# Loading alpha, q and k four tokens a run for the first nine units, and turning them by half-width products instead of transposes

## The chip, the cores and the metric

The kernel runs on one core of a Trainium2 chip. The metric is the device time of one execution in microseconds (us). Before the change the median of three executions is 540.11 us (539.74 to 540.44). The traces are of single executions taken by the hardware profiler; their clock starts at the span's start.

## The reference

Two stages. A gated linear attention over batch 4, heads 8, 768 tokens, head size 48, and then a feed-forward network on the 3072 rows of 384 channels that it makes.

```python
for t in range(S):
    state = alpha[:, :, t, :, None] * state + np.einsum('bhd,bhe->bhde', k[:, :, t], v[:, :, t])
    y[:, :, t] = np.einsum('bhd,bhde->bhe', q[:, :, t], state)
x = y.transpose(0, 2, 1, 3).reshape(B * S, H * D)
h = x @ w_in            # 384 -> 2048
g = np.maximum(0.01 * h, h)
out = g @ w_out         # 2048 -> 384
```

All is float32. alpha lies between 0.8 and 1.

## The kernel before, in words

**Units.** The tokens are cut into chunks of 128, and a unit is one chunk of one batch with its 8 heads: 24 units, numbered so that units 0 to 3 are the first chunk of the four batches, 4 to 7 the second, and so on. Three units make a block of 384 rows for the feed-forward network; there are 8 blocks. The first nine units (`AHEAD` = 9) run alone at the start, from 0 to about 60 us, since the network has nothing to do before block 0 is there; the later 15 units are strewn between the matrix products of the network.

**One unit.** alpha, q and k come from HBM, and must stand with the channel on the partition and the token along the free dimension, so that a running product over tokens is a scan along a row. In the first nine units the loads put a token on each partition and the 8 heads side by side (`by_token`, pitch 64 per head, 48 of them data and 16 ones); TensorE turns them: `transposed` issues four transposes of 128 columns, each of two heads, into one bank of PSUM (L272). In later units the load puts runs of four tokens on a partition and VectorE turns the data (L284), which the change does not touch. Then:

- `scans`: VectorE (DVE) makes the running product of alpha per head pair (`pc`, L309, four scans), reciprocals of every 16th (L311), and a scan backwards for the scaled inverses (`rc`, L315); GpSimd (POOL) copies two small columns (L319, L314).
- `scaled_q`, `scaled_k`: DVE multiplies the turned q by `pc` (L334) and the turned k by `rc` (L342).
- `scores`: eight products of 48 rows on TensorE (PE, L351), two at a time in the two halves of the array's rows, into an `a` and a `b` bank; ScalarE (ACT) copies them out (L361), POOL zeroes what lies above the diagonal (L362).
- `k_tokens`: four transposes of the scaled k (L374) and an ACT copy (L376).
- `outputs`: products of the state with q (only from unit 4 on), of the masked scores with v (L390; each has 64 or 48 stationary columns and they run in pairs, one in each half of the array's columns) and of k with v for the next state (L411). ACT rounds the result into the network's input (L419), DVE the remainder (L420).
- `next_state`: `us` (L430, L432) and the POOL product L367.

A float32 product is two passes and shows as two records in the trace; a transpose is one record.

**What sets the order.** The program writes units overlapped (`attention`): turning alpha of unit u+1 comes ahead of the scores of u, turning its q and k between the scores and the outputs of u. Within that, a list scheduler of the framework orders each engine's queue at build time by its own estimate of durations, so a change of instructions moves others too. Each engine executes its queue strictly in that order. Banks of PSUM come from two rotating sets of three (`a`, `b`). SyncE (SP) issues all loads; eight of them can be under way, since each takes one of eight semaphores in turn.

**Around the change.** Loads of alpha, q, k are double buffered: the load for u+2 waits until u has been turned. v has three buffers. The conversion of the network's weights from float32 words (ACT L238, L246; DVE L240, L243, L250, L252, L254, L257) starts inside the last of the nine units for f = 0 and 1. `keep_warm` issues products on zeros into an unused bank, so that PE isn't idle in the first 10 us: two per second transpose of alpha and q of unit 0, and for k of unit 0 two products of 512 and two of 256 columns (`keep_warm_wide`, L167). From about 76 us on, PE runs the network's products (L487, L512) nearly without a gap to the end.

## Time and profile before

| | |
|---|---|
| median of three executions | 540.11 us |
| profiled execution | 538.77 us, span 537.1 us, so 1.67 us outside the span |
| PE busy | 518.8 us, 97% of the span |
| DVE / ACT / POOL busy | 375.0 / 234.0 / 49.1 us |
| first nine units | 0 to about 60 us |
| time at which unit 1, 5, 6, 7, 8 begin their scan L309 | 9.86, 32.05, 39.15, 45.84, 52.78 us |
| loads of alpha, q, k of the first nine units | 192 KB each, runs of 192 bytes |

Busy time on PE counts a product from its start to its modelled end, and pipelined products overlap, so a step of the stream is read from the distance of starts and not from a duration. PE is the engine that matters after 76 us; before that, five engines wait for each other in a cycle per unit, and the distance between the same instruction of two successive units is the length of a cycle.

### The profile page before, as it was taken

What the parts mean: (1) busy time and instruction counts of PE and PEld (TensorE: products, weight loads), DVE (VectorE), ACT (ScalarE), POOL (GpSimd) and SP (SyncE); (2) the same over time, 40 slices, a digit from 0 to 9 for tenths busy, and PEclk for the clock granted to TensorE, in tenths of its full rate; (3) what the DMA queues carried; (4) which work ended last, traced back from release to release, by engine and by line L of the source; (5) the groups of instructions that cost most, each with busy time, mean ns of one, the idle gap of its engine ahead of it and who ended that gap; (6) DMA issues with size and microseconds to landing.
All of it is one profiled execution on the core that took longest, in us unless ns stands there. A gap on an engine that the chain in (4) does not pass through costs nothing.

```text
span 537.1 us, 10383 instructions
## 1 busy us (share of the span) xinstructions
PE 518.8 (97%) x3934; PEld 492.6 (92%) x3934; DVE 375.0 (70%) x703; ACT 234.0 (44%) x514; POOL 49.1 (9%) x116
## 2 busy tenths in 40 slices
PE   8879899999999999999999999999999999999995
PEld 7668789999999899999999999999999999999995
DVE  6778999999988897875675685775777534332331
ACT  2665755555533453435334443344343354233331
POOL 3333510000000011010000001000000000000000
PEclk9999899999999999999999999999999999999998
DMA  9999854454823643533323422523201010001001
GB/s 149 163 179 183 198 140 119 117 131 136 183 53 87 190 117 78 107 81 98 70 67 70 108 69 64 98 50 92 71 0 38 11 35 1 22 1 45 1 1 49
DMA packets 92985, 46.67 MB, mean 87 GB/s; under 512 B 57856, under 2 KB 90112, under 8 KB 92928
## 3 DMA queue, kind: packets, MB, share of 16 engines
q1 hardware_dynamic: 92928, 45.93, 39.0%
q8 instruction: 33, 0.54, 0.4%
q14 instruction: 24, 0.20, 0.1%
HBM read 38.83 MB, written 4.72 MB: 81 GB/s over the span
## 4 chain that ended last, share of the span: by engine, by line
PE 86%; DVE 4%; DMA 3%; issue 2%; ACT 1%; SPq 1%; POOL 1%; ACTq 0%; DVEq 0%; POOLq 0%
PE ph L487 36%; PE b L512 32%; PE a L390 5%; PE a L351 4%; PE a L512 4%; DMA small<-in_alpha_dram 2%; DMA raw<-in_moe_w_in_dram 1%; PE a L374 1%; PE b L272 1%; PE a L411 1%; PE b L390 1%; DVE pc L309 1%; PE b L411 1%; POOL sm L362 1%; DVE rc L315 0%
## 5 line engine op out<-in xcount | busy, mean ns | idle before, releaser
L487 PE MATMUL ph<-large,w 128*128 128x384 f32 x1152 | 227.4, 340 | 2.8 <-DVE t L493 2.8
L487 PEld LDWEIGHTS ph<-large,w 128*128 128x128 f32 x1152 | 201.9, 189 | 5.5 <-DVE t L493 3.9
L512 PE MATMUL b<-w,gh 128*128 128x384 f32 x672 | 170.0, 340 | 0.0
L493 DVE TENSOR_TENSOR t<-ph,t 128x384 f32<-128x384 f32 x128 | 70.5, 551 | 88.7 <-ACT t L490 88.4
L512 PEld LDWEIGHTS b<-w,gh 128*128 128x128 f32 x672 | 119.7, 188 | 2.2 <-issue 0.5
L490 ACT ACTIVATE t<-ph 128x384 f32<-128x384 f32 x128 | 62.6, 489 | 130.1 <-PE ph L487 122.8
L495 ACT CAST gh<-t 128x384 fp32r<-128x384 f32 x128 | 65.7, 514 | 112.8 <-DVE t L493 102.6
L512 PE MATMUL b<-w,gl 128*128 128x384 f32 x336 | 107.4, 336 | 0.0
L499 DVE TENSOR_TENSOR gl<-t,gh 128x384 fp32r<-128x384 f32 x128 | 70.8, 553 | 34.4 <-ACT gh L495 33.2
L512 PEld LDWEIGHTS b<-w,gl 128*128 128x128 f32 x336 | 62.5, 188 | 0.1
L362 POOL TENSOR_SCALAR_AFFINE_SELECT sm<-sm 128x512 f32<-128x512 f32 x33 | 22.8, 705 | 113.3 <-ACT sm L361 113.3
L351 PE MATMUL a<-qs,ks 48*128 48x128 f32 x312 | 30.9, 287 | 0.1
L351 PEld LDWEIGHTS a<-qs,ks 48*128 48x128 f32 x312 | 25.9, 189 | 5.4 <-issue 4.4
L284 DVE STREAM_TRANSPOSE ks<-small 128x512 f32<-128x512 f32 x15 | 16.6, 1121 | 12.3 <-PE a L374 12.3
L390 PE MATMUL a<-sm,small 128*48 128x128 f32 (+1 forms) x312 | 23.2, 282 | 0.1
L319 POOL COPY pe<-pc 128x4 f32<-128x4 f32 x24 | 4.8, 202 | 188.6 <-DVE pc L309 188.6
L309 DVE TENSOR_TENSOR_SCAN pc<-e,small 128x128 f32<-128x128 f32 x60 | 20.1, 398 | 0.5 <-ACT pc L327 0.5
L367 POOL TENSOR_TENSOR small<-us,pe 112x192 f32<-112x192 f32 x20 | 11.9, 594 | 90.2 <-DVE us L432 87.5
L390 PEld LDWEIGHTS a<-sm,small 128*48 128x48 f32 (+1 forms) x312 | 17.1, 132 | 3.2 <-issue 3.0
L361 ACT COPY sm<-a 128x512 f32<-128x512 f32 x24 | 14.0, 585 | 13.8 <-PE b L351 11.1
L512 PE MATMUL a<-w,gh 128*128 128x384 f32 x96 | 20.0, 336 | 0.0
L315 DVE TENSOR_TENSOR_SCAN rc<-e,small 128x511 f32<-128x511 f32 x15 | 19.0, 1270 | 0.2
(86 smaller groups left out, 525.4 us busy)
## 6 DMA issues: line engine op xcount, KB each, us to landing
raw<-in_moe_w_out_dram SPq DMA_DIRECT2D x16, 384.0 KB, 3.9
small<-in_v_dram SPq DMA_DIRECT2D x24, 192.0 KB, 4.0
raw<-in_moe_w_in_dram SPq DMA_DIRECT2D x32, 144.0 KB, 3.9
out_dram<-t SPq DMA_DIRECT2D x24, 192.0 KB, 1.9
small<-in_alpha_dram SPq DMA_DIRECT2D x32, 96.0 KB, 2.3
small<-in_q_dram SPq DMA_DIRECT2D x30, 96.0 KB, 2.2
small<-in_k_dram SPq DMA_DIRECT2D x30, 96.0 KB, 2.2
small<-in_alpha_dram SPq DMA_DIRECT2D x30, 80.0 KB, 2.3
```

Of the source, the lines that this page charges most:

```text
L284: nc.vector.transpose(t.rearrange("r p (j t) -> r p t j", t=T4), src.rearrange("r p (t d) -> r p t d", t=T4)[:, :, :, 0:32],)
L309: nc.vector.tensor_tensor_scan(pc[:, p, :], aT[:, p, :], ones.broadcast_to([P, C]), 1.0, ALU.mult, ALU.mult)
L315: nc.vector.tensor_tensor_scan(flat[2][:, NP * C - 2::-1], flat[0][:, NP * C - 1:0:-1], flat[1][:, NP * C - 2::-1], last, ALU.mult, ALU.add)
L351: nc.tensor.matmul(ss[s][:, p, :], ks[lo:lo + D, p, :], qs[lo:lo + D, p, :], start=True, stop=True)
L362: nc.gpsimd.affine_select(out=sm[s], in_=sm[s], compare_op=ALU.is_ge, fill=0.0, base=0, pattern=[[0, NP], [1, C]], channel_multiplier=-1)
L390: nc.tensor.matmul(y[s][HB * c:HB * c + lhsT.shape[-1], p % 2, :], lhsT, rhs, skip_group_check=True, **kw)
L487: nc.tensor.matmul(ph, w_in_of(f, wn, g), xt[:, g, :], start=n == 0, stop=n == 3 * NG - 1)
L490: put(ordered, "ACT", lambda: nc.scalar.mul(t, ph, 0.01))
L493: put(ordered, "DVE", lambda: nc.vector.tensor_tensor(t, ph, t, ALU.max))
L495: put(ordered, "ACT", lambda: nc.scalar.copy(gh, t))
L499: made["gl", i, f] = put(ordered, "DVE", lambda: nc.vector.tensor_tensor(gl, t, gh.bitcast(F32), ALU.subtract))
L512: nc.tensor.matmul(po[j], gt[:, js], w_out_of(f, wn), start=f == 0 and n == 0, stop=f == NF - 1 and n == 2)
```

## The change

For the first nine units each load of alpha, q or k becomes two loads (heads 0, 2, 4, 6 and heads 1, 3, 5, 7). A partition now holds four successive tokens of one head, 768 bytes in one run; partition 32p + j holds tokens 4j to 4j+3 of head pair p. The two halves of a tile lie `PITCH` = 208 elements apart, of which 16 at the end are ones (`tails`).

To turn such a tile, the kernel issues for each of the four tokens n of a run, and each half s, a product of 64 stationary columns (`src[:, at:at + HB]`: the 48 channels of that token and the 16 next elements) with the identity. The result goes into the PSUM partitions 64s to 64s+63 and into every fourth column, n, n+4, n+8 and so on, so that after the eight products column t of pair p is token t as before. It is a plain product, not a transpose, so each is two passes.

The zeros tile with its memset, and the wide products on it, are dropped; with k of unit 0 go four ordinary `keep_warm` products. The memset of the gaps on DVE covers 32 elements per row in place of 128, that of the rest on POOL 416 in place of 320.

```diff
         if u < AHEAD:
-            n = H if u or i else H // 2
-            for h in range(0, H, n):
+            for s in (0, 1):
                 nc.sync.dma_start(
-                    by_token(t)[:, h:h + n, 0:D], src[b, h:h + n, ts, :].rearrange("h t d -> t h d")
+                    t[:, s * PITCH:s * PITCH + RUN],
+                    src[b, s::2, ts, :].rearrange("p (j t) d -> p j (t d)", t=T4),
                 )
             return
...
-    zeros = cst.tile([P, 4 * C], F32R, name="zeros")
-    nc.gpsimd.memset(zeros.bitcast(F32), 0.0)
...
+    def tails(t):
+        return t[:, 0:2 * PITCH].rearrange("r (s n) -> r s n", s=2)[:, :, RUN:]
...
-            nc.vector.memset(by_token(t)[:, :, D:], 1.0)
+            nc.vector.memset(tails(t), 1.0)
...
-            nc.gpsimd.memset(t[:, H * HB:], 1.0)
+            nc.gpsimd.memset(t[:, 2 * PITCH:], 1.0)
...
         if u < AHEAD:
-            ps = banks4()
-            for p in range(NP):
-                last = nc.tensor.transpose(
-                    ps[:, p, :], by_token(src)[:, 2 * p:2 * p + 2, :].rearrange("t h d -> t (h d)"), ident
-                )
-                if u == 0 and p % 2:
+            ps = bank()
+            for n in range(T4):
+                for s in (0, 1):
+                    at = s * PITCH + n * D
+                    last = nc.tensor.matmul(
+                        ps[HB * s:HB * (s + 1), n::T4], src[:, at:at + HB], ident, start=True, stop=True, skip_group_check=True
+                    )
+                if u == 0 and n % 2:
                     with tc.issue_after(last.ins):
-                        if i == 2:
-                            keep_warm_wide(4 * C if p == 1 else 2 * C)
-                        else:
-                            keep_warm(2)
-            return ps
+                        keep_warm(2)
+            return ps.rearrange("r (p t) -> r p t", p=NP)
```

Since the scheduler orders the queues anew, more moves than the diff tells. Three places are shown. In a row, `L272 MATMUL a_113<-small_73 128x128 x2` is two instructions of line 272 that read the tile small_73 (all small tiles and the loads are parts of it) and write bank a_113; rows count program instructions, so a float32 product is one row here and two records in the trace. After the change line 272 is line 270, 162 is 160, 351 is 346, 374 is 369, 390 is 385, 411 is 406.

PE at the very start, up to the scores of unit 0. Before:

```order
L162 MATMUL ph_79<-small_73 128x128 x6
L272 MATMUL a_113<-small_73 128x128 x2
L162 MATMUL ph_79<-small_73 128x128 x2
L272 MATMUL a_113<-small_73 128x128 x2
L162 MATMUL ph_79<-small_73 128x128 x2
L272 MATMUL b_135<-small_73 128x128 x4
L272 MATMUL a_147<-small_73 128x128 x4
L272 MATMUL b_160<-small_73 128x128 x4
L162 MATMUL ph_79<-small_73 128x128 x4
L167 MATMUL ph_79<-zeros_77 128x512 x2
L167 MATMUL ph_79<-zeros_77 128x256 x2
L351 MATMUL a_178<-qs_145,ks_157 128x128
```

And of the change:

```order
L160 MATMUL ph_77<-small_73 128x128 x6
L270 MATMUL a_116<-small_73 64x128
L270 MATMUL b_143<-small_73 64x128
L270 MATMUL a_116<-small_73 64x128 x3
L160 MATMUL ph_77<-small_73 128x128 x2
L270 MATMUL a_116<-small_73 64x128 x4
L160 MATMUL ph_77<-small_73 128x128 x2
L270 MATMUL b_143<-small_73 64x128 x7
L270 MATMUL a_160<-small_73 64x128 x8
L270 MATMUL b_178<-small_73 64x128 x6
L160 MATMUL ph_77<-small_73 128x128 x8
L270 MATMUL b_178<-small_73 64x128 x2
```

The four banks that are turned here are alpha, q and k of unit 0 and alpha of unit 1. The first product of q stands between those of alpha, and the last two products of unit 1's alpha now stand behind eight `keep_warm` products.

PE in the cycle of unit 1, from the transposes of its scaled k on. Before:

```order
L374 MATMUL a_279<-small_73,ks_217 128x112 x4
L272 MATMUL b_288<-small_73 128x128 x4
L272 MATMUL a_296<-small_73 128x128 x4
L390 MATMUL b_304<-sm_272,small_73 64x128
L390 MATMUL b_304<-sm_272,small_73 48x128
L390 MATMUL b_304<-sm_272,small_73 64x128
L390 MATMUL b_304<-sm_272,small_73 48x128
L272 MATMUL b_331<-small_73 128x128 x4
L411 MATMUL b_304<-small_73,ktok_284 64x48
L411 MATMUL b_304<-small_73,ktok_284 48x48
```

And of the change:

```order
L369 MATMUL a_317<-small_73,ks_250 128x112 x4
L270 MATMUL a_339<-small_73 64x128 x2
L270 MATMUL b_326<-small_73 64x128 x8
L270 MATMUL a_339<-small_73 64x128 x6
L385 MATMUL b_352<-sm_310,small_73 64x128
L385 MATMUL b_352<-sm_310,small_73 48x128
L385 MATMUL b_352<-sm_310,small_73 64x128
L385 MATMUL b_352<-sm_310,small_73 48x128
L270 MATMUL b_379<-small_73 64x128
L406 MATMUL b_352<-small_73,ktok_322 64x48
L406 MATMUL b_352<-small_73,ktok_322 48x48
L385 MATMUL a_353<-sm_311,small_73 64x128
```

q and k of unit 2 (banks b_288, a_296, now b_326, a_339) take sixteen products in place of eight transposes. Of alpha of unit 3 (b_331, now b_379) one product stays where the four transposes were; the other seven now come behind the last L406, right ahead of the scores of unit 2.

DVE from the scaled k of unit 7 to that of unit 8, where the conversion of the weights f = 0 is mixed in. Before:

```order
L240 TENSOR_SCALAR bits<-raw 128x768
L243 SCALAR_TENSOR_TENSOR bits<-raw,bits 128x768
L309 SCALAR_TENSOR_TENSOR pc<-b,small 128x128 x4
L250 TENSOR_SCALAR pw<-bits 128x768
L310 MEMSET b 128x32
L311 RECIPROCAL small<-pc 128x32
L252 TENSOR_TENSOR bits<-bits,w_770 128x768
L254 SCALAR_TENSOR_TENSOR pw<-raw,pw 128x768
L315 SCALAR_TENSOR_TENSOR rc<-b,small 128x511
```

And of the change (L236 to L253 are L240 to L257 of before, L304 is L309, L415 is L420, L427 is L432):

```order
L236 TENSOR_SCALAR bits<-raw 128x768
L239 SCALAR_TENSOR_TENSOR bits<-raw,bits 128x768
L246 TENSOR_SCALAR pw<-bits 128x768
L415 TENSOR_TENSOR large<-a,large 112x2x128
L250 SCALAR_TENSOR_TENSOR pw<-raw,pw 128x768
L248 TENSOR_TENSOR bits<-bits,w_890 128x768
L304 SCALAR_TENSOR_TENSOR pc<-b,small 128x128 x4
L415 TENSOR_TENSOR large<-b,large 112x2x128
L427 TENSOR_TENSOR us<-small,b 112x192
L253 TENSOR_TENSOR w_890<-pw,bits 128x768
L305 MEMSET b 128x32
L306 RECIPROCAL small<-pc 128x32
```

The conversion now comes nearly whole ahead of unit 8's scan. In units 0 to 6 the two L420 of a unit, which before stood around the reciprocal L311 or behind the scan L315 of the next unit, now stand behind its L342. Behind unit 8 the queues of ACT, POOL and DVE are the same as before but for single neighbours.

More of the change, by code (lines that the diff above doesn't have):

```diff
@@ L162, in keep_warm @@
             nc.tensor.matmul(idle[:, 0:C], seed[:, 0, :], seed[:, 1, :], start=True, stop=True)
-    def keep_warm_wide(n):
-        for _ in range(2):
-            nc.tensor.matmul(idle[:, 0:n], zeros[:, 0:P], zeros[:, 0:n], start=True, stop=True)
     keep_warm(6)
+    def tails(t):
+        return t[:, 0:2 * PITCH].rearrange("r (s n) -> r s n", s=2)[:, :, RUN:]
     for i in (0, 1, 2):
         for t in loads_sb[i]:
-            nc.vector.memset(by_token(t)[:, :, D:], 1.0)
+            nc.vector.memset(tails(t), 1.0)
     for n in range(max(NL)):
```

## The prediction

> **What bounds the kernel now.** I began with the windows, cut where units 2, 3, 4, 5, 6, 7, 8 begin their scan L309 and where the network begins. The columns are the stretch, its length, the busy time of PE, PE's weight loads, DVE, ACT and POOL with their instructions, the granted clock of PE, the DMA share and GB/s.
>
> ```profile
> 15.21:20.82 5.61, 4.79 (x70) 3.92 (x69) 4.67 (x11) 3.75 (x10) 2.06 (x5) 1.00 1.30 154
> 26.43:32.05 5.62, 4.79 (x71) 3.92 (x69) 4.67 (x12) 3.80 (x11) 2.06 (x5) 1.00 0.92 187
> 32.05:39.15 7.10, 5.11 (x76) 3.98 (x75) 4.88 (x12) 3.94 (x11) 2.07 (x5) 1.00 0.99 173
> 39.15:45.84 6.69, 6.69 (x84) 5.97 (x82) 5.16 (x13) 3.94 (x11) 2.10 (x5) 0.75 1.21 180
> 45.84:52.78 6.94, 6.63 (x109) 5.61 (x108) 6.72 (x14) 3.56 (x11) 2.38 (x5) 1.00 0.90 178
> 45.84:69.91 24.07, 22.22 (x280) 18.70 (x278) 22.91 (x44) 15.79 (x39) 9.53 (x13) 0.93 0.92 202
> 76.40:537.10 460.70, 453.05 (x3192) 436.61 (x3192) 312.19 (x568) 192.98 (x416) 22.82 (x56) 1.00 0.30 73
> ```
>
> From 76.4 us PE is busy for 453.05 of 460.70 us, with work that the change leaves alone. So the change is worth what it moves the 76.4 us, no more and no less. Ahead of that no engine is full in a cycle of 5.61 us, and the DMA share is around 1 (overlapping packets count twice). The waits of 15 to 33 us say who holds the cycle:
>
> ```profile
> DVE pc L309 <- PE b L272: 3.6, 4, 1.0
> PE b L390 <- POOL sm L362: 2.5, 3, 0.8
> ```
>
> The two alternate: PE waits 0.8 us a cycle for POOL's masked scores, DVE 0.9 us for the turned alpha, which stands behind that wait in PE's queue. One cycle of PE and its ends, from the timeline (start, length, engine, line):
>
> ```profile
> 20.06 0.66 PE L272 MATMUL b<-small 128*128 128x128 f32 x4
> 20.64 0.61 PE L411 MATMUL b<-small,ktok 128*64 128x48 f32 x15
> 20.82 1.36 DVE L309 TENSOR_TENSOR_SCAN pc<-b,small 128x128 f32<-128x128 f32 x4 [0.86 <-PE b L272]
> 21.05 0.30 PE L390 MATMUL a<-sm,small 128*48 128x128 f32 x1
> 21.69 0.37 PE L351 MATMUL a<-qs,ks 48*128 48x128 f32 x1
> 22.57 0.27 PE L351 MATMUL a<-qs,ks 48*128 48x128 f32 x1
> 22.78 0.60 PE L374 MATMUL a<-small,ks 112*128 112x112 f32 x4
> 23.22 0.60 PE L272 MATMUL b<-small 128*128 128x128 f32 x4
> 23.66 0.60 PE L272 MATMUL a<-small 128*128 128x128 f32 x4
> 25.09 0.65 PE L390 MATMUL b<-sm,small 128*64 128x128 f32 x8 [0.83 <-POOL sm L362]
> ```
>
> Starts give the steps: four transposes 0.44 us (23.22 to 23.66), 0.58 with the change of shape behind them (20.06 to 20.64). The scores, eight products in pairs, two passes each, are eight steps of 0.107 with 0.21 for the first, and 1.09 to the next kind (21.69 to 22.78).
>
> **What is removed, added, moved.**
>
> *The new turn.* Eight products of two passes, in pairs on the two halves of the columns. No row shows one. The nearest is L390: the same 64 stationary columns, 128 moving ones, 128 rows, in pairs:
>
> ```profile
> 50.06 0.32 PE L390 MATMUL b<-qs,small 48*64 48x128 f32 x2
> 50.67 0.66 PE L272 MATMUL b<-small 128*128 128x128 f32 x4
> 51.26 0.65 PE L390 MATMUL b<-sm,small 128*64 128x128 f32 x8
> 51.74 0.27 PE L411 MATMUL b<-small,ktok 128*48 128x48 f32 x4
> ```
>
> Eight records take 0.48 us to the next kind (51.26 to 51.74): four steps of 0.107 and 0.05, against 0.15 behind transposes. So a bank costs 16 records, 0.86 us, for 0.44: 0.42 more on PE, 27 times. Bounds: a pair that doesn't overlap costs 1.72 a bank; cheaper than 0.86 no row allows. I take 0.86, the row being the same form but for the strided target.
>
> *A cycle of the first chunk* (units 1 to 4 in the scans; PE only): scores 1.09, L374 0.54, q and k 16 steps and a first step 1.81, switch 0.05, L390 0.48, one product of alpha alone 0.26 (two steps and a switch), first L411 0.10, L390 0.48, rest of L411 0.32, seven products of alpha 1.03 (0.21, six steps of 0.107, and 0.18 to the scores). Sum 6.16. POOL's wait is gone: its result lets L390 go 3.40 us after the scores begin (21.69 to 25.09), and PE's own queue now comes to L390 after 1.09 + 0.54 + 1.81 + 0.05 = 3.49. DVE, busy 4.67 us a cycle, is not full. So PE becomes the bound: 4 × 6.16 = 24.64 us against 22.19 from 9.86 to 32.05: **+2.45**. Bounds: 5.61, if it doesn't push (+0.25), to 6.57, if each switch costs the 0.15 to 0.20 of the transposes (+4.1).
>
> *Cycles with a state* (units 4 and 5): scores 1.09, L374 0.54, q and k 1.81, switch 0.05, state products 0.58 (0.61 at 50.06), L390 0.91, L411 0.43, alpha 1.04: 6.45. Before they took 7.10 and 6.69. The first held ACT in a wait for weights, the second ran at clock 0.75:
>
> ```profile
> ACT raw L238 <- DMA raw<-in_moe_w_in_dram: 2.6, 1, 2.6
> DMA to landing us min/median/max: 2.4/4.9/7.4
> DMA to landing us min/median/max: 1.9/2.2/3.8
> L128 SPq DMA_DIRECT2D small<-in_q_dram x9: 378/912/2311, 1.9 to 49.3; - x9
> L135 SPq DMA_DIRECT2D small<-in_q_dram x60: 311/430/1652, 136.4 to 384.6; - x60
> ```
>
> The last four rows are the loads' landing and SP's issue, of L128 (192-byte runs) and of L135 (768-byte runs, the new form). Two loads at 0.43 cost SP what one at 0.91 did, and in the cycle of 6.2 us SP's six and one v fit; but they land in 2.2 and not 4.9 us, so the weights, which stand behind v of unit 5 on SP, are there before ACT asks. With PE full I take clock 1.00. 2 × 6.45 − 13.79 = **−0.89** (bounds −1.6 at 6.1 a cycle, +1.9 if one of them runs at 0.75, 6.45 / 0.75 = 8.6).
>
> The Trainium skill, "TensorE: Matmul & The Clock Gate", Part 4, says that transposes don't count as activity for the clock gate as products do; by it the new products would make the 0.75 stretch less likely. The stretch of 15.21 to 32.05 has 36 transposes at 1.00, so the rows don't show it; by the rule −0.89 stands, without it +1.9 is open.
>
> *The start.* The rows of before:
>
> ```profile
> 4.25 0.64 PE L272 MATMUL a<-small 128*128 128x128 f32 x2
> 4.68 0.75 PE L162 MATMUL ph<-small 128*128 128x128 f32 x4
> 5.27 0.38 PE L272 MATMUL a<-small 128*128 128x128 f32 x2
> 5.69 1.36 DVE L309 TENSOR_TENSOR_SCAN pc<-a,small 128x128 f32<-128x128 f32 x4 [3.36 <-PE a L272]
> 8.17 1.06 PE L162 MATMUL ph<-small 128*128 128x128 f32 x8
> 8.98 0.94 PE L167 MATMUL ph<-zeros 128*128 128x512 f32 x4
> 9.86 1.35 DVE L309 TENSOR_TENSOR_SCAN pc<-b,small 128x128 f32<-128x128 f32 x4
> 10.00 0.37 PE L351 MATMUL a<-qs,ks 48*128 48x128 f32 x1
> ```
>
> PE begins at 4.25 either way, when the first six keep-warm products are through. Steps take 0.21 there up to about 5.3, and 0.11 behind. Alpha of unit 0 needs about ten steps (the first three products don't pair) and four of L160 (0.6 with switches): 4.25 + 1.05 + 0.55 + 0.6 + 0.2 to the reader = 6.65, against 5.69. Then, on PE: the other L160 0.6, q 0.96, k 0.86, six of alpha 0.65, eight L160 of two records 1.9, two of alpha 0.3, so the scores begin near 11.7 and the scan of unit 1 with them, against 9.86 to 10.00. Through DVE (6.65 and the 4.2 us from the first scan to the second) it would be 10.9. What hides the wide products today (PE waits for DVE's L342 until 10.00) doesn't hide the new L160, since alpha stands behind them. I take **+1.6** (bounds +0.4, if loads and pairing give half of it back, to +2.0).
>
> *Waits for loads that vanish.* The second cycle lost 1.2 us to alpha of unit 2, of this in all:
>
> ```profile
> PE b L272 <- DMA small<-in_alpha_dram: 1.7, 2, 1.2
> ```
>
> Its cycle of 5.35 is in the 22.19 already, and PE's 6.16 stands over it. So the gain is swallowed. The Trainium skill, "DMA: Bandwidth & Descriptors", Specifications, gives 512 bytes as the least size for full rate; by it alone the loads would be the gain, −1.7 us from this row. The 2.2 against 4.9 us agree on the loads, not on the path.
>
> *The conversions.* From unit 7's scan (45.84) to the end of the second L499 (69.91) DVE is busy 22.91 of 24.07 us. The same instructions now come in another order, with the conversion ahead of unit 8's scan. The most that a late start can win back is 1.16, all of DVE's idle time; I take **−0.8** (bounds −1.16 to 0). Behind it, DVE goes on full, and PE waits for it until 76.4.
>
> The memsets, on POOL and DVE ahead of 3.7 us, lie beside the first keep-warm products; uncovered they would cost 0.6 us.
>
> **Sum**: 1.6 + 2.45 − 0.89 − 0.8 = +2.36, so 2.4. The profiled execution would be 538.77 + 2.4 = 541.2; it lies 1.34 under the median of 540.11. On the median: **542.5 us**. All low bounds together give −2.1 (0.4 + 0.25 − 1.6 − 1.16), all high ones +8.0 (2.0 + 4.1 + 1.9); the latter needs three at once.
>
> **Rivals.**
>
> 1. *Faster: the room that PE has in a cycle takes the new products.* Place: the wait for POOL ahead of L390, 0.83 us, with 0.15 per switch that the equal shape of the turn and L390 saves. It decides if PE's cycle comes to 5.55, its mean today. Then 0.9 − 0 − 1.6 − 0.8 = −1.5: 538.6. For it: PE waits 0.83 today and is busy 4.79 of 5.61. Against it: 3 × 0.42 is 1.26, more than 0.83. Chance 0.15.
> 2. *No change: half of it.* The start costs 0.9 (through DVE only), the cycles 5.8 (+1.0) and 6.25 (−1.3), the conversions give 0.8: −0.2, 539.9. For it: the long DVE path of the start. Chance 0.23.
> 3. *The pairs don't overlap*, through the strided target or the shared identity: 0.86 more a bank, 3 × 0.86 × 6 cycles and 4 × 0.86 at the start, some 19 on the forecast: 561. Against it: L390 pairs. Chance 0.04.
> 4. The loads may not be what is waited for at all; that is in the forecast.
>
> **How the numbers follow.** The forecast has 0.58. A measurement of this kernel tells about 0.2% (1.08 us) from no change. Above +1.08 lie the forecast and rival 3, 0.62 less what of the forecast falls short of 1.08, say 0.03, and 0.01 of rival 2; I say 0.60 slower. Within: 0.24. Below −1.08: 0.16. The range runs from −0.8 (into rival 2 and the edge of rival 1) to +4.7 (forecast with one more high bound): 539.3 to 544.8. The forecast's own is 541.2 to 544.8.
>
> **What would show it.** The distance of unit scans L304 in the first chunk: 6.1 to 6.3 confirms, 5.6 is rival 1, over 8 rival 3. PE's wait for POOL ahead of L385 gone, a new wait of DVE's L304 for PE. A group L270 of 432 records, whose steps are 0.107 a pair. The first scan at 6.4 to 6.8 and the second at 11 to 12; at 10 the start was misjudged. No wait of ACT L234 for weights. Wrong altogether, if the network's steady run begins ahead of 76.4.

## The result, and the profile after

The changed kernel takes 568.98 us, the median of four executions (567.77 to 569.65). The kernel before takes 539.92 us on the same chip (538.89 to 540.44). The ratio is 1.054, with a 95% interval of 1.051 to 1.056. Slower was forecast, but by 2.4 us; it is 29 us, and the time lies 24 us above the upper end of the range. The profiled execution took 568.45 us (before: 538.77).

From the page of the changed kernel (span 566.7 us), the rows in 40 slices for the DMA engines: busy tenths, and what they moved in GB/s.

```profile
DMA  2344467444465165334333233143211010001001
GB/s 81 104 123 110 128 148 192 115 130 113 117 180 123 26 187 140 93 79 82 106 73 87 51 108 90 28 87 91 68 42 35 1 43 1 22 0 44 0 1 47
```

A slice is 14 us. Through the first five of them, 71 us, the DMA engines are busy to two to four tenths and they move 81 to 128 GB/s. The loads of alpha, q and k of the first eight units are all issued there; the six loads of the ninth follow from 71.72 to 76.4 us.

The windows of the changed kernel (columns as in the prediction: stretch, length, PE, its weight loads, DVE, ACT and POOL, granted clock, DMA share, GB/s), cut at the scans L304 of units 1 and 2, 3 and 4, 4 and 5, and at the network's steady run:

```profile
0.00:10.00 10.00, 7.54 (x34) 5.59 (x35) 0.74 (x8) 1.28 (x1) 3.40 (x14) 1.00 0.20 65
16.94:22.75 5.81, 5.81 (x102) 5.38 (x102) 4.86 (x11) 3.44 (x9) 1.54 (x4) 1.00 0.40 109
29.11:39.06 9.95, 7.67 (x102) 6.95 (x102) 5.06 (x12) 3.76 (x10) 2.05 (x5) 0.83 0.44 114
39.06:55.53 16.47, 10.50 (x152) 8.79 (x152) 5.03 (x13) 4.46 (x11) 2.05 (x5) 1.00 0.47 122
105.37:566.70 461.33, 453.04 (x3192) 436.63 (x3192) 312.00 (x568) 193.54 (x416) 22.82 (x56) 1.00 0.28 73
```

The first of these stretches, 0 to 10 us, in the kernel before:

```profile
0.00:10.00 10.00, 7.88 (x49) 7.15 (x49) 5.54 (x18) 1.28 (x1) 3.74 (x17) 1.00 1.01 138
```

The steady run now begins at 105.37 us, where it began at 76.40, and takes 461.33 us to the end of the span for 460.70. So the loss lies ahead of it. In the first 10 us the DMA share fell from 1.01 to 0.20 and the rate from 138 to 65 GB/s. That is with no engine of the core full: DVE is busy for 0.74 us of the ten.

The unit scans on DVE (units 0, 1, 4, 5 and 7 of the changed kernel):

```profile
10.14 1.37 DVE L304 TENSOR_TENSOR_SCAN pc<-a,small 128x128 f32<-128x128 f32 x4 [8.42 <-PE a L270]
...
16.94 1.36 DVE L304 TENSOR_TENSOR_SCAN pc<-b,small 128x128 f32<-128x128 f32 x4 [1.21 <-PE b L270]
...
39.06 1.37 DVE L304 TENSOR_TENSOR_SCAN pc<-b,small 128x128 f32<-128x128 f32 x4
...
55.53 1.36 DVE L304 TENSOR_TENSOR_SCAN pc<-b,small 128x128 f32<-128x128 f32 x4
...
70.85 1.36 DVE L304 TENSOR_TENSOR_SCAN pc<-b,small 128x128 f32<-128x128 f32 x4
```

From unit 1 to unit 2 the cycle is 5.81 us, with PE full. From unit 4 to unit 5 it is 16.47. The first products of the turn, on PE's timeline, and two of the waits up to 90 us (total, times, longest):

```profile
4.62 0.66 PE L270 MATMUL a<-small 128*64 128x128 f32 x2 [0.16 <-DMA small<-in_alpha_dram]
...
6.75 1.12 PE L270 MATMUL a<-small 128*64 128x128 f32 x6 [0.40 <-DMA small<-in_alpha_dram]
```

```profile
ACT raw L234 <- DMA raw<-in_moe_w_in_dram: 11.5, 2, 10.8
...
PE a L270 <- DMA small<-in_k_dram: 8.3, 7, 2.3
```

PE takes each new tile of the start when its load lands. ACT waits once for 10.8 us, for weights. Pieces of the chain of waits (start, length) show which transfers set the end:

```profile
2.24 4.46 DMA small<-in_alpha_dram
...
38.82 6.49 DMA small<-in_alpha_dram
...
50.10 3.49 DMA raw<-in_moe_w_in_dram
...
76.38 7.86 DMA small<-in_k_dram
```

The load that is issued at 2.24 us lands 4.46 us later, and later ones take 6.49 and 7.86 us. ACT's wait is behind them. SP issues the weights' loads L198 from 46.50 us on, behind the slow loads in its own order, and L234 gets its data at 53.69:

```profile
53.69 0.88 ACT L234 ACTIVATE raw<-raw 128x768 f32<-128x768 f32 x1 [10.76 <-DMA raw<-in_moe_w_in_dram]
```

```profile
L198 SPq DMA_DIRECT2D raw<-in_moe_w_in_dram x64: 312/564/2355, 46.5 to 162.6; - x64
```

Behind L234 on ACT stand the casts L414 of the unit in hand, so a unit's cycle stops with it. That is the 16.47 us.

### The profile page after: what moved, and what is told of

Its sections match the earlier page's. It is cut to its first block, busy times and chain, and to the rows that moved or that the text cites. A ratio compares the mean times of both kernels' runs of the same rounds, so it can differ in the third digit from the quotient of the medians.

```text
span 566.7 us, 11062 instructions
## 1 busy us (share of the span) xinstructions
PE 539.6 (95%) x4262; PEld 511.1 (90%) x4262; DVE 375.3 (66%) x703; ACT 234.5 (41%) x514; POOL 48.2 (9%) x115
## 4 chain that ended last, share of the span: by engine, by line
PE 86%; DMA 6%; DVE 3%; SPq 1%; issue 1%; ACT 1%; ACTq 0%; DVEq 0%
PE ph L482 34%; PE b L507 31%; PE a L385 6%; PE a L346 4%; PE a L507 4%; PE b L270 3%; DMA small<-in_k_dram 2%; DMA small<-in_alpha_dram 2%; PE a L270 2%; DMA raw<-in_moe_w_in_dram 1%; PE a L369 1%; PE b L385 1%; SPq L198 1%; PE a L406 1%; PE ph L160 1%
## 5 line engine op out<-in xcount | busy, mean ns | idle before, releaser
L482 PE MATMUL ph<-large,w 128*128 128x384 f32 x1152 | 226.1, 338 | 2.9 <-DVE t L488 2.9
L482 PEld LDWEIGHTS ph<-large,w 128*128 128x128 f32 x1152 | 200.7, 188 | 5.6 <-DVE t L488 3.8
L488 DVE TENSOR_TENSOR t<-ph,t 128x384 f32<-128x384 f32 x128 | 70.5, 551 | 88.0 <-ACT t L485 87.8
L270 PE MATMUL b<-small 128*64 128x128 f32 x272 | 25.5, 305 | 2.6 <-DMA small<-in_alpha_dram 2.1
L415 DVE TENSOR_TENSOR large<-a,large 112x256 fp32r<-112x256 f32 x39 | 15.2, 417 | 17.2 <-ACT large L414 17.2
L270 PE MATMUL a<-small 128*64 128x128 f32 x160 | 18.1, 317 | 8.9 <-DMA small<-in_k_dram 8.3
L279 DVE STREAM_TRANSPOSE ks<-small 128x512 f32<-128x512 f32 x15 | 16.7, 1127 | 13.3 <-PE a L369 13.3
L270 PEld LDWEIGHTS b<-small 128*64 128x64 f32 x272 | 19.8, 155 | 5.0 <-issue 2.5
L270 PEld LDWEIGHTS a<-small 128*64 128x64 f32 x160 | 13.5, 160 | 11.7 <-DMA small<-in_k_dram 6.6
L385 PE MATMUL a<-sm,small 128*64 128x128 f32 (+1 forms) x312 | 23.9, 282 | 0.0
L414 ACT CAST large<-a 112x256 fp32r<-112x256 f32 x39 | 13.6, 372 | 24.6 <-PE a L385 24.2
L362 POOL TENSOR_TENSOR small<-us,pe 112x192 f32<-112x192 f32 x20 | 13.2, 660 | 124.3 <-DVE us L427 90.2
```

What stands on the lines that cost most here:

```text
L270: last = nc.tensor.matmul(ps[HB * s:HB * (s + 1), n::T4], src[:, at:at + HB], ident, start=True, stop=True, skip_group_check=True)
L279: nc.vector.transpose(t.rearrange("r p (j t) -> r p t j", t=T4), src.rearrange("r p (t d) -> r p t d", t=T4)[:, :, :, 0:32],)
L385: nc.tensor.matmul(y[s][HB * c:HB * c + lhsT.shape[-1], p % 2, :], lhsT, rhs, skip_group_check=True, **kw)
L415: made["x", u] = nc.vector.tensor_tensor(xl, y[s][0:BR], xh.bitcast(F32), ALU.subtract)
L482: nc.tensor.matmul(ph, w_in_of(f, wn, g), xt[:, g, :], start=n == 0, stop=n == 3 * NG - 1)
L488: put(ordered, "DVE", lambda: nc.vector.tensor_tensor(t, ph, t, ALU.max))
```

## The experiments

**Theory 1** says that a load whose outermost dimension is four is carried by four of the sixteen DMA engines. The changed loads have the four heads outermost; those of the kernel before have 128 tokens there. **Theory 2** blames the number of loads, 54 in place of 28, with SP's issue and the semaphores. **Theory 3** blames the new products on PE and the order that they force. The kernels that were compared:

| kernel | loads of the first nine units | turn | median us | ratio to before, 95% |
|---|---|---|---|---|
| before | 128 tokens outermost, 192-byte runs | 4 transposes | 539.92 | |
| after | 4 heads outermost, 768-byte runs | 8 products | 568.98 | 1.051 to 1.056 |
| e1 | 32 runs outermost, 768-byte runs | 8 products | 546.41 | 1.010 to 1.016 |
| e2 | 8 heads outermost, 768-byte runs | 8 products | 546.55 | 1.010 to 1.016 |
| e3 | as before | 8 products | 545.58 | 1.007 to 1.013 |
| e4 | as after | 4 transposes | 565.81 | 1.046 to 1.052 |
| e5 | as e1 | 4 transposes | 542.62 | 1.003 to 1.007 |
| e6 | as e1, no keep-warm products between | 8 products | 545.25 | 1.007 to 1.012 |
| e7 | as before, two loads a tensor and unit | 4 transposes | 539.62 | 0.999 to 1.002 |
| e8 | 2 heads outermost, 768-byte runs | 8 products | 625.78 | one execution |
| e9 | as e1, one DVE step less ahead of the network | 8 products | 543.84 | 1.006 to 1.011 |
| e10 | as before, one DVE step more there | 4 transposes | 541.01 | 1.003 to 1.006 |

### e1: the same loads, with the runs outermost

```diff
-                    src[b, s::2, ts, :].rearrange("p (j t) d -> p j (t d)", t=T4),
+                    src[b, s::2, ts, :].rearrange("p (a t) d -> a p (t d)", a=JA, t=T4),
...
-                        ps[HB * s:HB * (s + 1), n::T4], src[:, at:at + HB], ident, ...
+                        ps[HB * s:HB * (s + 1), n::T4], src[:, at:at + HB], turn, ...
```

`JA` is 32. `turn` is an identity with its columns in the order of the rows; two instructions on POOL at the start make it.

> Only the loads of the first nine units differ from the changed kernel: the same 768-byte runs, the same number of loads, but the 32 runs of four tokens are the outermost dimension of the source and the four heads the inner one. A partition then holds another run, and a permuted identity in the new products puts the columns back; order and number of instructions on every engine but POOL (two more at the start) are the same. Theory 1 (a load whose outermost dimension is four is carried by four of the sixteen DMA engines: the changed kernel shows a share of 0.20 and 65 GB/s in its first 10 us) expects a share of 0.5 or more and 120 GB/s or more there, the first scan L304 near 6.7 us, the network's steady run near 78 us and 540 to 545 us. Theory 2 (twice as many loads: their issue on SP and the semaphores they share) expects no change, 566 to 571, since the loads are as many. Theory 3 (the new products on PE and the order that they force) expects 566 to 571 too.

Measured: 546.41 us (544.1 to 550.08), 22.6 less than the changed kernel. Its windows, and the group of its loads of alpha with the landing times of all of them:

```profile
0.00:10.00 10.00, 8.47 (x72) 7.49 (x74) 3.00 (x16) 1.28 (x1) 5.05 (x18) 1.00 0.45 118
19.01:24.85 5.84, 5.84 (x102) 5.41 (x102) 4.84 (x12) 3.76 (x10) 2.05 (x5) 1.00 0.60 144
```

```profile
L127 SPq DMA_DIRECT2D small<-in_alpha_dram x18: 535/555/1587, 0.8 to 48.9; - x18
...
DMA to landing us min/median/max: 2.4/2.8/5.7
```

The share is 0.45, a little under what theory 1 asked, the rate 118 GB/s for 65, and a load lands in 2.8 us (median), where the chain of the changed kernel shows 4.46, 6.49 and 7.86. The long wait of ACT is gone, since the weights' loads begin at 31.0 us instead of 46.5:

```profile
L198 SPq DMA_DIRECT2D raw<-in_moe_w_in_dram x64: 312/564/1822, 31.0 to 138.2; - x64
```

But for the two on POOL, the instructions, their order and the number of loads are those of the changed kernel. So 22.6 of the 29 us hang on which dimension of the source is outermost. Theories 2 and 3 fall as explanations of that part. The time is still above the 540 to 545 that theory 1 and my sum allowed, with the first scan at 7.66 us for 6.7 and the steady run at 80.69 for 78; e3, e6 and e9 follow that up.

### e2 and e8: eight and two outermost

```diff
-                    src[b, s::2, ts, :].rearrange("p (j t) d -> p j (t d)", t=T4),
+                    src[b, :, tb * C + s * HB:tb * C + (s + 1) * HB, :].rearrange("h (j t) d -> h j (t d)", t=T4),    # e2
+                    src[b, 2 * s:2 * s + 2, tb * C:tb * C + 2 * C, :].rearrange("h (j t) d -> h j (t d)", t=T4),      # e8
```

> The changed kernel with the outermost dimension of its loads at eight: a load takes half of the unit's tokens for all eight heads, 8 x 16 runs of 768 bytes, where the changed kernel takes all tokens for four heads, 4 x 32 runs. Size, number and order of the loads and all other instructions are the same; rows land under other heads and tokens than the products take them for, so what is computed is not the reference. Theory 1: six loads of a unit are 590 KB; over four engines at the 65 GB/s of the start that is 9.1 us a unit, over eight engines 4.5 us, less than PE's cycle of about 6.2; so most of the loss goes, with some 1 to 2 us left at the start: 542 to 549 us, DMA share near 0.4 in the first 10 us. Theory 2 and theory 3 expect 566 to 571.

> The changed kernel with the outermost dimension of its loads at two: each takes two heads of 256 tokens, 2 x 64 runs of 768 bytes; size, number and order of the loads and all other instructions are the same, rows land under other heads and tokens than the products take them for, so what is computed is not the reference. Theory 1: the 590 KB of a unit took 8.65 us a unit over four engines (first to ninth scan of the changed kernel, 69.2 us for eight), so 17.3 over two: the ninth scan comes near 155 us where it came at 79, and the time is 620 to 660 us; DMA share near 0.12 and some 35 GB/s in the first 10 us. Theories 2 and 3 expect 566 to 571.

Measured: 546.55 us (545.94 to 547.44) with eight, 625.78 us with two. The first 10 us of e8 and of e2, and the first and the ninth scan of e8:

```profile
0.00:10.00 10.00, 4.28 (x16) 3.21 (x16) 0.74 (x8) 1.28 (x1) 3.40 (x14) 1.00 0.10 31
```

```profile
0.00:10.00 10.00, 8.47 (x66) 7.33 (x68) 2.65 (x15) 1.28 (x1) 3.75 (x16) 1.00 0.36 106
```

```profile
13.59 1.37 DVE L304 TENSOR_TENSOR_SCAN pc<-a,small 128x128 f32<-128x128 f32 x4 [11.86 <-PE a L270]
...
130.62 1.37 DVE L304 TENSOR_TENSOR_SCAN pc<-b,small 128x128 f32<-128x128 f32 x4 [0.27 <-PE b L270]
```

With 2, 4, 8 and 32 outermost the share is 0.10, 0.20, 0.36 and 0.45, and the rate 31, 65, 106 and 118 GB/s. Twice the dimension is twice the rate from two to four, 15.5 and 16.3 GB/s for each unit of it, and 13.3 at eight; times sixteen, the shares are 1.6, 3.2, 5.8 and 7.2 busy engines. The traces show the parts of a load more directly, by the rises of the semaphore that tells of its landing. Behind the first load of alpha it rises 2 times in e8 (5.57 and 5.70 us), 4 times in the changed kernel (4.12 to 4.49), 8 times in e2 (3.28 to 3.80) and 16 times in e1 and in the kernel before (3.00 to 3.43 and 2.70 to 3.17), for 96 KB each time; in the first three it also rises once at the issue. So the load ends in as many parts as theory 1 says. At eight the loads are no longer what holds the cycle, and more engines bring nothing further. With two, a unit takes (130.62 − 13.59) / 8 = 14.6 us, less than the 17.3 that I had scaled from four; the total fell into the range all the same. The four kernels do the same loads in number and size, so theories 2 and 3, which expected 566 to 571 for each, are out.

### e3 and e4: the two halves of the change apart

e3 has the loads of before and the new products; the tile is by token again, and the target is not strided:

```diff
-                    at = s * PITCH + n * D
+                    at = (2 * n + s) * HB
...
-                        ps[HB * s:HB * (s + 1), n::T4], src[:, at:at + HB], ident, ...
+                        ps[HB * s:HB * (s + 1), n * C:(n + 1) * C], src[:, at:at + HB], ident, ...
```

> The loads of the kernel before (a token a partition, 192-byte runs, one load a tensor and unit) with the new turn by eight products of half the columns, two at a time, each head's into its own 128 columns of the bank. The loads' outermost dimension is 128. Theory 1 and my sum for PE and the start expect 540.5 to 545 us, first scan near 6.7 us, second 11 to 12, unit scans 6.1 to 6.3 us apart in the first chunk. Theory 3 (the products are what costs) expects 560 or more. Theory 2 expects the same as theory 1.

e4 has the loads of after and four transposes a tile:

```diff
-            for n in range(T4):
-                for s in (0, 1):
-                    ...
+            for n in range(T4):
+                at = n // 2 * PITCH + n % 2 * D
+                last = nc.tensor.transpose(ps[:, n * C:(n + 1) * C], src[:, at:at + P], ident)
```

> The loads of the changed kernel (four heads outermost) with the turn of the kernel before, four transposes of 128 columns a tile. The transposes then turn runs of four tokens of one head as if they were two heads, so what is computed is not the reference; the work is the same in size. Theory 1 expects the loss to stay: 562 to 572 us, DMA share near 0.20 in the first 10 us, and the same waits for loads of k and alpha on PE. Theory 2 expects the same. Theory 3 expects 538 to 545.

Measured: 545.58 us (544.04 to 546.66) and 565.81 us (564.36 to 566.7). The scans of units 0 to 3 in e3, and the first 10 us of e4:

```profile
6.70 1.37 DVE L303 TENSOR_TENSOR_SCAN pc<-a,small 128x128 f32<-128x128 f32 x4 [4.37 <-PE a L269]
...
12.44 1.36 DVE L303 TENSOR_TENSOR_SCAN pc<-b,small 128x128 f32<-128x128 f32 x4 [1.48 <-PE b L269]
...
18.28 1.37 DVE L303 TENSOR_TENSOR_SCAN pc<-b,small 128x128 f32<-128x128 f32 x4
...
24.24 1.37 DVE L303 TENSOR_TENSOR_SCAN pc<-b,small 128x128 f32<-128x128 f32 x4
```

```profile
0.00:10.00 10.00, 6.14 (x30) 4.84 (x30) 3.20 (x16) 1.28 (x1) 3.78 (x16) 1.00 0.20 64
```

The loads alone cost 26 us (565.81 for 539.92) and the products alone 5.7 (545.58). Theory 3, which expected 538 to 545 of e4 and 560 or more of e3, is out; e4 has the share of the changed kernel, 0.20. With both halves the loss is 29.1, a little less than the sum of the two, 31.6. (e3 also has the change's keep-warm products, so the 5.7 holds their part.) The first two scans of e3 come at 6.70 and 12.44, where I had worked out 6.65 and 11 to 12, and the cycles are 5.84 and 5.96 us, where I had 6.16.

### e5 and e7: the long runs without the fault, and the number of loads

e5 is e4 with the source of e1. e7 splits the loads of before by heads:

```diff
-            n = H if u or i else H // 2
+            n = H // 2
```

> The loads of e1 (768-byte runs, two loads a tensor and unit, the 32 runs outermost) with the turn of the kernel before, four transposes a tile; rows and columns land in other places than the transposes take them for, so what is computed is not the reference, and the work is the same in size. It differs from e4 only in which of the source's dimensions is outermost. Theory 1 (four engines): the 23 us of e4 go, and the time is that of the kernel before within 2 us, 538 to 542; DMA share 0.4 to 0.5 in the first 10 us. Theory 2 (the number of loads) expects 560 or more, as in e4. My prediction's step on the loads (their gain is swallowed by the cycle that DVE, PE and POOL hold) expects within 1 us of the kernel before; if the longer runs alone were worth what alpha's wait of 1.7 us showed, 1.7 less.

> The kernel before with each of its loads of alpha, q and k in the first nine units split in two by heads, 0 to 3 and 4 to 7: 54 loads where there were 28, all of 192-byte runs with the 128 tokens outermost, as in the changed kernel two for each tensor and unit; every engine but SP does the same in the same order. Theory 1 expects no change, 538 to 542. Theory 2 (number of loads, SP, semaphores) expects 550 or more.

Measured: 542.62 us (540.43 to 544.21) and 539.62 us (539.12 to 540.98).

Twice as many loads cost nothing in e7 (ratio 0.9987 to 1.0019), so theory 2 is out from this side too. The DMA share of e5 in the first 10 us is 0.50 for 0.20 in e4. Turning the source's dimensions takes 23.2 us off e4. The long runs gain nothing: e5 is 0.5% above the kernel before (1.003 to 1.007), not below it, and 0.6 us above the 538 to 542 that theory 1 allowed. The prediction's "the gain is swallowed" holds in that there is no gain. What the 0.5% is made of stays open; e5 also lacks the wide keep-warm products of the kernel before, and no run separates the two.

### e6: the start without keep-warm products

```diff
-                if u == 0 and n % 2:
+                if False and n % 2:
```

> e1 without the keep-warm products that stand behind the turned banks of unit 0: 24 records of L160 between 5.86 and 12.75 us of e1, 3.9 us of PE (1.14 + 0.71 + 2.05). If they are what puts the second scan at 13.20 and not at the 11.7 that I had worked out, it comes at 10.5 to 11.5 and the time falls by 1.5 to 2.5 us against e1, 543.5 to 545. If alpha or k of unit 1 is what is waited for at the start, the second scan stays within 0.5 us of 13.2 and so does the time. If the clock falls without them (granted clock below 0.95 between 10 and 30 us), the time rises.

Measured: 545.25 us (544.5 to 545.45), 1.2 less than e1, less than the 1.5 to 2.5 asked. The second scan comes at 10.36 us instead of 13.20, but the third at 18.07 for 19.01. The window says where the rest went:

```profile
10.00:20.00 10.00, 9.50 (x128) 8.72 (x130) 7.15 (x19) 4.55 (x12) 2.31 (x7) 0.83 0.70 168
```

The granted clock is 0.83 in this stretch, where e1 has 1.00. So e6 is 2.8 us ahead at the second scan and loses 1.9 of it in the next cycle, at the lower clock, behind a stop of PE of 1.51 us (8.98 to 10.50). The 2.8 is not the price of the products alone, since PE's steps fall from 0.21 to 0.107 us at 5.1 us in e6 and at 6.7 in e1. The intervals of the two ratios overlap, so the gain in time is not clear of noise.

### e9 and e10: the clock behind PE's wait ahead of the network

In e1 PE stands ahead of the steady run and waits for DVE's L488, the end of the first network columns. The windows (the work before it, the wait, and the stretch up to the next nine products L482):

```profile
72.50:78.34 5.84, 5.84 (x35) 5.84 (x34) 5.10 (x11) 2.92 (x6) 1.09 (x1) 1.00 0.27 68
78.34:80.69 2.35, 0.34 (x2) 0.02 (x1) 2.32 (x4) 0.17 (x1) 0.00 (x0) 1.00 0.20 55
80.69:85.51 4.82, 4.82 (x19) 4.82 (x20) 4.79 (x8) 3.34 (x6) 0.00 (x0) 0.65 0.42 140
```

The third stretch takes 4.82 us at clock 0.65; before the change the same work took 3.24 us (76.41 to 79.65) at 1.00, behind a wait of 1.29. e9 leaves one DVE step out of e1, e10 adds one to the kernel before:

```diff
-        put(ordered, "DVE", lambda: nc.vector.tensor_tensor(val, val, hi.bitcast(F32), ALU.subtract))
+        f == EARLY or put(ordered, "DVE", lambda: nc.vector.tensor_tensor(val, val, hi.bitcast(F32), ALU.subtract))    # e9
...
-        made["w", f] = put(ordered, "DVE", lambda: nc.vector.tensor_tensor(lo, rest, val, ALU.add))
+        for _ in range(2 if ordered and f == EARLY else 1): made["w", f] = put(...)                                    # e10
```

> e1 with one DVE step left out: the subtraction L248 of the conversion of weights ahead of the network (0.96 us at 77.35 in e1); the low half of those weights is then wrong, and nothing else changes but the order of the last steps on DVE. In e1, e3 and e6 PE stands still for 2.3 us ahead of the network's steady run, waiting for DVE, and the granted clock of the 4.8 us behind it is 0.65 (before: 1.2 us of waiting, and 1.00 for 3.24 us). If the length of that wait is what lets the clock fall, PE now waits 1.3 us, the nine products L482 and what follows them to the next nine take 3.2 instead of 4.8 us, and the time falls by 0.96 + 1.6, 2.5 us against e1: near 544. If the dip comes from elsewhere, it stays, and the time falls by 1.0 at most.

> The kernel before with one DVE step more at the same place: the last addition L257 of that conversion is made twice (0.96 us; the result is the same). If the length of PE's wait lets the clock fall, PE waits 2.2 us ahead of the steady run in place of 1.2, the clock is near 0.65 for the next 4.8 us, and the time rises by 0.96 + 1.6: 542 to 543. If not, the clock stays at 1.00 there and the time rises by 1.0.

Measured: e9 543.84 us (542.99 to 544.16), 2.6 less than e1 (by the ratios to the kernel before, 1.0085 and 1.013, 2.4 us). Its windows:

```profile
73.02:78.90 5.88, 5.88 (x36) 5.85 (x34) 5.20 (x11) 2.95 (x6) 1.09 (x1) 1.00 0.27 63
78.90:80.26 1.36, 0.29 (x2) 0.00 (x0) 1.36 (x3) 0.13 (x1) 0.00 (x0) 1.00 0.34 108
80.26:83.50 3.24, 3.24 (x18) 3.24 (x19) 3.21 (x6) 2.79 (x5) 0.00 (x0) 1.00 0.67 197
```

The wait is 1.36 us, the clock behind it 1.00, and the three stretches together take 10.48 us where e1 took 13.01: 2.53 less, for a step of 0.96. So the shorter wait was worth another 1.57 us here. (The intervals of the two ratios overlap; it is the stretches that show it.)

e10 is inconclusive. Its time rose by 2.1 us (541.01 against 538.9), but the wait that it was to lengthen did not come about, and at the place meant the clock is 1.00. PE stopped earlier, for POOL, and the clock fell behind that stop:

```profile
67.48 0.65 PE L390 MATMUL a<-sm,small 128*64 128x128 f32 x8 [1.58 <-POOL sm L362]
```

```profile
65.77:69.18 3.41, 1.83 (x29) 1.34 (x30) 2.28 (x4) 2.21 (x8) 2.25 (x2) 1.00 0.76 220
69.18:72.59 3.41, 3.41 (x22) 3.32 (x17) 3.01 (x6) 1.36 (x3) 1.09 (x1) 0.50 0.40 98
77.14:80.42 3.28, 3.28 (x18) 3.28 (x19) 3.25 (x6) 2.82 (x5) 0.00 (x0) 1.00 0.55 120
```

The first two rows are cut where the trace's own record of the granted clock is: it consists of pieces at 1.00 and at 0.50, each 3.41 us long or a multiple of it. The 0.65 of e1 is such a piece at 0.50 (81.87 to 85.28) and a rest at 1.00. The length of a stop alone does not tell whether the clock falls. PE's idle time within one piece of 3.41 us tells it better:

| kernel | PE stops, us | idle within the piece | clock of the next piece |
|---|---|---|---|
| e1 | 78.68 to 80.69 (2.01) | 2.01 | 0.50 |
| e10 | 65.91 to 67.48 (1.58) | 1.58 | 0.50 |
| e6 | 8.98 to 10.50 (1.51) | 1.51 | 0.50 |
| e2 | 40.75 to 42.62 (1.87) | 1.46 | 1.00 |
| e9 | 40.08 to 41.70 (1.61) | 1.42 | 1.00 |

In the first 180 us of the twelve traces, 28 pieces at 1.00 have 1.5 us or more of PE idle, and 27 of them are followed by 0.50. Of 536 with less, two are (1.45 us in the kernel before, 1.36 in e4). This is read off the traces; no run moved only the idle time of a piece.

## Why the prediction was right and wrong

The account goes by the step's ends on DVE: the scans of units 1, 5 and 7, and the L488 (before: L493) for which PE waits ahead of the steady run. Rows of the changed kernel, of the kernel before and of e1 (scans of units 1, 5 and 7, and L488), from DVE's timeline:

```profile
104.76 0.55 DVE L488 TENSOR_TENSOR t<-ph,t 128x384 f32<-128x384 f32 x1
```

```profile
75.81 0.55 DVE L493 TENSOR_TENSOR t<-ph,t 128x384 f32<-128x384 f32 x1
```

```profile
13.20 1.37 DVE L304 TENSOR_TENSOR_SCAN pc<-b,small 128x128 f32<-128x128 f32 x4 [1.21 <-PE b L270]
...
37.89 1.35 DVE L304 TENSOR_TENSOR_SCAN pc<-b,small 128x128 f32<-128x128 f32 x4
...
50.81 1.36 DVE L304 TENSOR_TENSOR_SCAN pc<-b,small 128x128 f32<-128x128 f32 x4
...
80.08 0.55 DVE L488 TENSOR_TENSOR t<-ph,t 128x384 f32<-128x384 f32 x1
```

| step | predicted | after | e1 |
|---|---|---|---|
| start, to the scan of unit 1 (before: 9.86) | +1.6 | +7.08 | +3.34 |
| four cycles to the scan of unit 5 (22.19) | +2.45 | +16.40 | +2.50 |
| two cycles with a state (13.79) | −0.89 | +1.53 | −0.87 |
| to PE's wait for L488 (75.81 − 45.84 = 29.97) | −0.8 | +3.94 | −0.70 |
| behind it, to the next nine products (79.65 − 75.81 = 3.84) | 0 | 0.00 | +1.59 |
| sum | +2.36 | +28.95 | +5.86 |

(After: 16.94, 55.53, 70.85, 104.76, 108.60. e1: 13.20, 37.89, 50.81, 80.08, 85.51.)

**The step that failed** is the one on loads. It took landing (2.2 us) and issue (0.43 us) of the new loads from the group L135, because both have 768-byte runs, and concluded that the weights would be there before ACT asks. The run length is not what sets it. L135 has 32 runs outermost, the new L127 four heads. With four outermost the loads moved 65 GB/s and landed in 4.5 us with few others under way, in 6.5 and 7.9 later; ACT then waited 10.8 us for weights. With 32 outermost the same runs land in 2.8 us and are issued in 0.56, near what the step had assumed. The change of this one dimension moves 22.6 us. The step had also set loads of 192 KB against loads of 96 KB: in e7, 96 KB in 192-byte runs land in 3.7 us (median), so 1.2 of the 2.7 us between 4.9 and 2.2 came with the size. Among the rivals there was none in which the loads become the bound, so the range could not reach the time.

The Trainium skill, "DMA: Bandwidth & Descriptors", "Why a DMA increments its semaphore by 16 and not by 1", states the rule: a transfer uses the largest number of engines up to sixteen that divides the slowest dimension (other than one) of both access patterns. The traces agree, with 2, 4, 8 and 16 rises of the semaphore for 2, 4, 8 and 32 or 128 outermost, and with shares of 0.10, 0.20 and 0.36 of sixteen engines for 2, 4 and 8; they do not show which engines these are. The prediction had weighed that page's 512 bytes and not this rule, which speaks against the change.

**The price of a bank** was right. A bank is 16 records (27 banks, 432 in all; the first two rows are of the changed kernel), and the pairs overlap: in e1 (the last two rows) sixteen records take 0.88 us, from 20.79 to 21.67, eight steps of 0.11, where the sum had 0.86.

```profile
L270 PE MATMUL b<-small 128*64 128x128 f32 x272 | 25.5, 305 | 2.6 <-DMA small<-in_alpha_dram 2.1 <-DMA small<-in_q_dram 0.4
L270 PE MATMUL a<-small 128*64 128x128 f32 x160 | 18.1, 317 | 8.9 <-DMA small<-in_k_dram 8.3 <-DMA small<-in_alpha_dram 0.6
...
20.79 1.04 PE L270 MATMUL b<-turn,small 128*64 128x128 f32 x16
21.67 0.82 PE L270 MATMUL a<-turn,small 128*64 128x128 f32 x12
```

In e1 a cycle of the first chunk is 5.84 us with PE busy for all of it: PE does become the bound, but the sum of 6.16 had counted 0.32 too many, 0.20 of it behind the first four L385, where products of alpha, L406 and L385 alternate (22.76 to 24.75 in e1, 1.99 us for 2.19). That the four cycles came to +2.50 is partly chance. Three took 5.81 to 5.85, and the fourth 7.19, because ACT's wait for weights now falls there (1.45 us in e1), where the kernel before had it a unit later. Against the prediction such a wait is still there. PE's long wait for POOL ahead of L385 went, as it said. DVE does not wait for PE in its place; it waits 0.8 us a cycle for ACT's L414.

**The cycles with a state** took 6.46 us each in e1, where the sum had 6.45, at clock 1.00 as assumed. PE fills only the second of them; in the first it is busy for 5.68 us and waits 0.78 for DVE's L310, so that one's match is chance.

**The conversions** gave 0.70 where 0.8 was predicted, but not for the reason given. DVE's idle time, which was to be won back, hardly changed: 1.35 us before (29.97 − 28.62) and 1.28 in e1 (29.27 − 27.99):

```profile
45.84:75.81 29.97, 27.77 (x310) 23.92 (x307) 28.62 (x53) 17.80 (x42) 10.61 (x14) 0.94 0.79 174
...
50.81:80.08 29.27, 26.90 (x338) 23.28 (x336) 27.99 (x50) 16.93 (x38) 8.98 (x14) 1.00 0.63 154
```

DVE has less to do there, 50 instructions for 53: two steps L420 and the L432 behind them (48.90 to 49.90 before) now stand ahead of unit 7's scan, in cycles that PE holds. The number was met by luck.

**The start** was sized too low by 1.0 us in e3 (+2.58) and 1.7 in e1, and the slow loads make it +7.08. PE's queue was followed rightly up to the first scan, 6.70 for 6.65 in e3. Behind it the prices hold too (in e3 the keep-warm products take 0.64, 0.64 and 1.98 us for the sum's 0.6, 0.6 and 1.9), but five products of alpha, not two, stand behind the last of them in e3 (0.80 us for 0.3), and the prediction took +1.6 where its own queue gave 1.7 to 1.8. e1 has the predicted order. It is 1.0 us late at the first scan already (7.66), in the main because PE's steps stay at 0.21 us up to 6.7 us, where in e3 they are 0.107 from 5.3 on. In the changed kernel they stay at 0.21 up to 12.7, so its +7.08 holds slow products as well as slow loads. The clock's record begins only there (4.97 us before, 5.20 in e3, 6.77 in e1, 12.72 after), so a 1.00 in a window ahead of it is not a measured clock.

**Not foreseen** was the clock behind PE's wait: 1.59 us in e1, none in the changed kernel itself, whose steady run begins behind a wait of 1.38 us at clock 1.00.

**The rivals.** The first (faster, PE has room) fell: with the loads mended the change still costs 6.5 us in e1 and 5.7 in e3. The second (no change) fell with it. The third (pairs don't overlap) fell on the 0.107 us a step. So without the fault of the loads the forecast of 542.5 would have been 3.9 us low, and inside no range that I gave: its upper end was 544.8. One bound was worked out wrongly as well: 8.6 + 6.45 − 13.79 is +1.26 and not the +1.9 given, and the range's +4.7 follows from no single high bound (+4.0 with that of the first cycles, +4.5 with this one); neither would have reached the time.

## What to carry to other kernels

When a load is rewritten, compare its whole access pattern with that of the load from which its landing is taken: how many items the outermost dimension has, not only how long the runs are. Here a turn of two dimensions, with a permuted identity to undo it in the products, was worth 22.6 us. None of the mended forms beats the kernel before: with the loads spread, the longer runs bring nothing, and two passes in place of one on PE cost 4 to 6 us (3.8 from e5 to e1; 5.7 from the kernel before to e3, with the change's keep-warm products).

## What the hardware did that I had not expected

- A DMA's rate followed the number of items in its outermost dimension: 31, 65 and 106 GB/s with 2, 4 and 8, at the same size and run length, and its semaphore rose 2, 4 and 8 times at the landing.
- The granted clock fell to 0.65 for 4.8 us behind a PE wait of 2.3 us, and stayed at 1.00 behind 1.3 to 1.4 us there. The Trainium skill, "TensorE: Matmul & The Clock Gate", Part 1, has the clock halve behind an idle window of about 3.4 us and come back behind a busy one as long. Half the clock for 3.4 of 4.8 us would be 0.65 on the mean: an estimate from that page, which agrees with the measured record (0.50 for 3.41 us). The idle window does not agree: 2.01 us of PE idle within such a piece were enough, and 1.51 in e6.
- The stretch from 20 to 70 us has a granted clock of 0.93, 0.90, 0.90 and 0.96 in the kernels with four transposes and quick loads (before, e5, e7, e10) and of 1.00, 1.00, 0.97, 1.00 and 1.00 in those with eight products (e1, e2, e3, e6, e9). That is the way in which the Trainium skill's rule on transposes, named in the prediction, points, by little between e10 and e3; but the products also fill PE more (48.5 of 50 us in e1, 44.5 before), and no run holds that apart.
